# Another order of the same instructions in a linear attention with a two-layer feed-forward behind it

## The chip, the cores and the metric

The kernel runs on one core of a Trainium2 chip. The metric is the device time of one execution in microseconds. A NeuronCore has a matrix engine (TensorE, PE in the profile; its weight loads are PEld), VectorE (DVE), ScalarE (ACT), GpSimd (POOL) and a sync engine (SP) that here only issues DMAs. Each engine takes its own instructions in program order; semaphores hold them to each other.

## The reference

The first half is a linear attention with a decaying state, for 4 batches, 8 heads, 768 positions and a head size of 48:

```
for t in range(S):
    kt, vt, rt, wt = (k[:, :, t], v[:, :, t], r[:, :, t], w[:, :, t])
    cur = np.einsum('bhd,bhe->bhde', u[None] * kt, vt)
    y[:, :, t] = np.einsum('bhd,bhde->bhe', rt, state + cur)
    state = wt[:, :, :, None] * state + np.einsum('bhd,bhe->bhde', kt, vt)
```

The second half takes y as x (3072 rows of 384) through `h = np.maximum(x @ w_in, 0.0)` with w_in of 384 x 2048, and `h * h @ w_out` with w_out of 2048 x 384. All data are float32.

## The kernel before, in words

The sequence is cut into 6 chunks of 128 positions. A unit is one chunk of one batch; c1b3 below stands for chunk 1, batch 3. All weights stay on the chip.

**Weights.** There are 8 blocks, w0 to w7, each with a half of w_in (`wi`, 768 numbers in each of 128 partitions) and one of w_out (`wo`). SP loads them (L416, L418). Each matrix product is made of three: a number is split into a lead, which the fast matrix format holds, and the rest. Per half block that takes one ACT copy (L429), three VectorE operations (shift L433, sign L437, low L442), one ACT copy of the lead (L449) and one subtraction on POOL (L450).

**Attention of a unit.** SP loads w, k, r (L472) and v (L505). From chunk 2 on VectorE transposes blocks (L481, the steps z0 and z1 for two batches together) and SP spreads them into the tile `pt` (L491); before, PE transposes. VectorE makes the running product of w (scan, four of L536), r times it (rt, L554) and three products for k (kn L560, kn2 L561, kq L564). In chunks 1 to 4 the diagonal terms come from POOL (rk L586, ru L588), a VectorE sum (L591), three small VectorE maxima (bh, L594 to L596) and ACT (diag, L632). PE turns k (ktp, L637), and ACT copies it (L639). Then comes one long PE step, "mix" of a unit: L670 (through the state), L679 and L652 (scores and outer products of the next unit), L689. After it VectorE adds the state (S L699, S2 L702) and masks the next unit's scores (mask, L711), ACT and VectorE split the result into lead and rest (x L613, xl L616), SP sends parts to other partitions (L727), and ACT clears the accumulator (zero, L824).

**Feed-forward.** A position in it is a number, two steps of which (28, 30, ...) are one block of 128 of the 2048 hidden columns for four batches (for chunk 1 and part of chunk 0 for two batches). Per block: hp on PE (L862, nine matmuls), g1 on ACT (L867), g2 (ACT L869 in chunk 0, VectorE L871 after), g3 on ACT (L873), g4 on VectorE (L874, the rest of the squared hidden values), and ob on PE (L880, three matmuls per batch). There are two buffers for hp and three for g.

**What sets the order.** Every step is added with its reads and writes (class Plan, `add`). The numbers of all 2451 steps stand in a table ORDER in the order in which they are emitted (`order`, `run`); each engine executes its share in that order. PLACES names a buffer for each slot, FILLS puts idle transposes on PE ahead of some early steps. ORDER, PLACES and FILLS are handed over in one line:

```
P.table = ORDER, PLACES, FILLS
with tc.manual_schedule():
    P.run()
```

Of the kernel before, what the change touches and what calls it, by code (L numbers as in the profile page):

```python
# [96 lines left out]
class Names:  # L97
# [121 lines left out]
)  # L219
FILLS = {  # L220
    17: (3, 'ob', 1), 16: (3, 'ob', 2), 56: (3, 'ob', 1), 57: (4, 'ob', 1), 42: (3, 'ob', 1), 49: (2, 'ob', 1), 83: (3, 'ob', 3), 90: (18, 'ob', 1),
    160: (4, 'ob', 0), 469: (2, 'ob', 0), 128: (2, 'side', 0), 130: (3, 'side', 0), 192: (7, 'side', 0),
}

# [796 lines left out]
```

## Time and profile before

| what | value |
|---|---|
| median of 3 runs | 528.38 us (526.41 to 528.43) |
| the profiled execution | 528.06 us |
| its span, first to last instruction | 526.3 us, mean granted clock 0.992 |
| PE busy | 506.8 us (96%), 5425 matmuls |
| PEld busy | 457.3 us (87%) |
| DVE busy | 368.8 us (70%), 799 instructions |
| ACT busy | 319.0 us (61%) |
| POOL busy | 98.6 us (19%) |

Busy shares are means over the span. VectorE and ScalarE work hardest in the first 130 us, in which the weights are split and chunks 0 and 1 and the start of chunk 2 of the attention are made; PE has no gap in many later stretches. So the question for each stretch is which engine PE waits for there.

### The profile page before, as it was taken

What the parts mean: (1) busy time and instruction counts of PE and PEld (TensorE: products, weight loads), DVE (VectorE), ACT (ScalarE), POOL (GpSimd) and SP (SyncE); (2) the same over time, 40 slices, a digit from 0 to 9 for tenths busy, and PEclk for the clock granted to TensorE, in tenths of its full rate; (3) what the DMA queues carried; (4) which work ended last, traced back from release to release, by engine and by line L of the source; (5) the groups of instructions that cost most, each with busy time, mean ns of one, the idle gap of its engine ahead of it and who ended that gap; (6) DMA issues with size and microseconds to landing.
All of it is one profiled execution on the core that took longest, in us unless ns stands there. A gap on an engine that the chain in (4) does not pass through costs nothing.

```text
span 526.3 us, 13737 instructions
## 1 busy us (share of the span) xinstructions
PE 506.8 (96%) x5425; PEld 457.3 (87%) x5425; DVE 368.8 (70%) x799; ACT 319.0 (61%) x870; POOL 98.6 (19%) x141
## 2 busy tenths in 40 slices
PE   8999998989999999999998999999999999999995
PEld 7888887768999999988987998889988888998894
DVE  6899889999687899878778667678467354333232
ACT  5898888877775867666574556564543353423232
POOL 2025741734204040220403000402100000000000
PEclk9899999998999999999999999999999999999999
DMA  8989799502657756466672481661171010100001
GB/s 164 226 196 232 163 224 203 126 16 48 106 110 97 146 89 105 91 112 105 93 153 32 72 147 18 102 121 40 25 138 36 1 20 6 57 17 0 1 0 65
DMA packets 188312, 48.74 MB, mean 93 GB/s; under 512 B 178001, under 2 KB 183122, under 8 KB 188242
## 3 DMA queue, kind: packets, MB, share of 16 engines
q1 hardware_dynamic: 187664, 47.01, 46.8%
q8 instruction: 44, 0.72, 0.6%
q10 hardware_dynamic: 578, 0.79, 0.4%
q14 instruction: 26, 0.21, 0.1%
HBM read 31.66 MB, written 4.72 MB: 69 GB/s over the span
## 4 chain that ended last, share of the span: by engine, by line
PE 78%; DVE 9%; SPq 6%; DMA 3%; ACT 2%; issue 1%; POOL 0%; DVEq 0%; POOLq 0%
PE ob L880 34%; PE hp L862 33%; PE ob L670 2%; SPq L505 2%; PE ob L689 2%; SPq L416 2%; DMA ri<-in_moe_w_in_dram 2%; PE a L679 2%; DVE q L442 1%; PE a L652 1%; DMA ro<-in_moe_w_out_dram 1%; DVE g L874 1%; SPq L472 1%; PE hp L637 1%; DVE q L437 1%
## 5 line engine op out<-in xcount | busy, mean ns | idle before, releaser
L880 PE MATMUL ob<-wo,g 128*128 128x384 f32 x1152 | 229.5, 342 | 5.3 <-DVE g L874 2.9
L862 PE MATMUL hp<-x,wi 128*128 128x512 f32 (+1 forms) x1062 | 221.9, 354 | 4.0 <-DVE g L874 2.3
L880 PEld LDWEIGHTS ob<-wo,g 128*128 128x128 f32 x1152 | 200.3, 189 | 14.5 <-DVE g L874 3.8
L862 PEld LDWEIGHTS hp<-x,wi 128*128 128x128 f32 x1062 | 174.3, 188 | 30.6 <-DVE g L874 3.3
L871 DVE SCALAR_TENSOR_TENSOR hp<-hp,t 128x512 f32<-128x512 f32 (+1 forms) x96 | 58.1, 606 | 74.1 <-ACT t L867 73.8
L867 ACT ACTIVATE t<-hp 128x512 f32<-128x512 f32 (+1 forms) x118 | 60.9, 517 | 67.1 <-PE hp L862 42.3
L874 DVE TENSOR_TENSOR g<-hp,g 128x512 fp32r<-128x512 f32 (+1 forms) x118 | 68.9, 585 | 37.5 <-ACT g L873 37.0
L873 ACT CAST g<-hp 128x512 fp32r<-128x512 f32 (+1 forms) x118 | 59.6, 507 | 48.9 <-DVE hp L871 47.9
L660 POOL MEMSET S<- 1x1 f32 x20 | 1.8, 88 | 238.9 <-PE ob L670 238.9
L632 ACT ACTIVATE m<-diag,beta 128x64 f32<-128x64 f32 x160 | 40.3, 337 | 2.6 <-DVE beta L595 2.6
L616 DVE SCALAR_TENSOR_TENSOR x<-ob,x 112x128 fp32r<-112x128 f32 x80 | 21.1, 283 | 18.9 <-ACT x L613 16.6
L824 ACT COPY ob<-zero 112x128 f32<-112x128 f32 x80 | 20.6, 268 | 19.1 <-DVE x L616 9.6
L613 ACT ACTIVATE x<-ob 112x128 fp32r<-112x128 f32 x80 | 19.2, 277 | 20.3 <-PE ob L689 14.6
L536 DVE TENSOR_TENSOR_SCAN pt<-pt,zero 112x128 f32<-112x128 f32 x64 | 27.1, 455 | 2.6 <-DMA pt<-st 1.0
L586 POOL TENSOR_TENSOR st<-st 128x384 f32<-128x384 f32 x20 | 22.6, 1134 | 32.8 <-DVE st L481 22.7
L450 POOL TENSOR_TENSOR wi<-q,wi 128x768 fp32r<-128x768 f32 x8 | 17.0, 2128 | 45.1 <-ACT wi L449 32.7
L588 POOL TENSOR_TENSOR st<-st,un 128x384 f32<-128x384 f32 x20 | 21.8, 1096 | 1.2
L481 DVE STREAM_TRANSPOSE st<-st 128x1152 f32<-128x1152 f32 x16 | 21.6, 1362 | 0.0
L554 DVE TENSOR_TENSOR pt<-pt 112x508 f32<-112x508 f32 x24 | 21.0, 877 | 0.6 <-ACT pt L522 0.4
L543 ACT ACTIVATE m<-pt 112x512 f32<-112x512 f32 x24 | 15.2, 632 | 9.1 <-DVE pt L536 7.8
L450 POOL TENSOR_TENSOR wo<-q,wo 128x768 fp32r<-128x768 f32 x8 | 15.7, 1961 | 26.0 <-ACT wo L449 26.0
L561 DVE SCALAR_TENSOR_TENSOR m<-pt,m 112x512 f32<-112x512 f32 x24 | 18.2, 760 | 0.3
(121 smaller groups left out, 542.8 us busy)
## 6 DMA issues: line engine op xcount, KB each, us to landing
pt<-st SPq DMA_DIRECT2D x96, 96.0 KB, 2.9
ro<-in_moe_w_out_dram SPq DMA_DIRECT2D x8, 768.0 KB, 6.0
v<-in_v_dram SPq DMA_DIRECT2D x96, 48.0 KB, 2.8
out_dram<-q SPq DMA_DIRECT2D x20, 192.0 KB, 2.0
ri<-in_moe_w_in_dram SPq DMA_DIRECT2D x32, 96.0 KB, 4.7
ri<-in_moe_w_in_dram SPq DMA_DIRECT2D x8, 384.0 KB, 6.0
st<-in_w_dram SPq DMA_DIRECT2D x8, 384.0 KB, 4.9
st<-in_k_dram SPq DMA_DIRECT2D x8, 384.0 KB, 4.6
```

The costliest lines, as they stand in the source:

```text
L450: P.add("pool", 1.9, rank(8 * k + 5), lambda q=q, tt=tt: G.tensor_tensor(out=tt[:, 1], in0=q.tile, in1=tt[:, 0].bitcast(F32), op=ALU.subtr ...
L481: V.transpose(out=zt[:, i].rearrange("a t p q i -> a t (p q) i"), in_=sv[:, :, i].rearrange("s t p q x -> s t (p q) x"))
L536: lambda p=p: V.tensor_tensor_scan(out=pt[:, 0, p], data0=src(0)[:, p], data1=zero.broadcast_to([HP, C]), initial=1.0, op0=ALU.mult, op1=A ...
L586: P.add("pool", 0.97, rank("rk"), lambda: G.tensor_tensor(out=rk(), in0=rk(), in1=vals(2), op=ALU.mult), r=[(st, ui, 2)], w=[(st, ui, 1)])
L588: P.add("pool", 0.97, rank("ru"), lambda: G.tensor_tensor(out=rk(), in0=rk(), in1=un.rearrange("s (h d) -> s h d", d=D), op=ALU.mult), r=[ ...
L632: A.activation(M.tile[:, o:o + Q], diag2, AF.Copy, scale=beta.tile[:, i:i + 1])
L862: T.matmul(hp.tile[:, 0:n], wi[f][:, wl, kt], xT[:, kt, xl, xs], start=(m == 0), stop=(m == 3 * KT - 1))
L867: P.add("act", 0.49 if full else 0.28, rank("g1"), lambda: A.activation(t(), h(), AF.Relu), r=[hp], w=[(g, 1)])
L871: P.add("dve", 0.605 if full else 0.337, rank("g2"), lambda: V.scalar_tensor_tensor(out=h(), in0=h(), scalar=0.0, in1=t(), op0=ALU.max, op ...
L873: P.add("act", 0.48 if full else 0.26, rank("g3"), lambda: A.copy(out=hi(), in_=h()), r=[hp], w=[(g, 0)])
L874: P.add("dve", 0.605 if full else 0.335, rank("g4"), lambda: V.tensor_tensor(out=lo(), in0=h(), in1=hi().bitcast(F32), op=ALU.subtract), r ...
L880: T.matmul(obs[b][:, 0:DM], g.tile[0][:, gl, o:o + C], wo[f][:, wl], start=(f == 0 and m == 0), stop=(f == NF - 1 and m == 2))
```

## The change

Only the three tables differ. Every step stays on its engine with the same operation and shape; the emission order changes, and with it which buffer a slot gets. The last 690 of the 2451 numbers of ORDER are the same, from the mix of chunk 4, batch 1 on. The steps that follow differ in the first 320 us or so of the program. FILLS has 56 idle transposes in place of 57, at other places. One row of ORDER and the whole of FILLS in the diff:

```
 ORDER = (
-    5, 15, 19, 21, 7, 6, 17, 16, 315, 0, 11, 20, 18, 8, 13, 24, 25, 26, 27, 22, 23, 28, 1, 10, 314, 9, 56, 62, 2, 31, 60, 32, 33, 12, 93, 58, 29, 316, 65, 30,
...
 FILLS = {
-    17: (3, 'ob', 1), 16: (3, 'ob', 2), 56: (3, 'ob', 1), 57: (4, 'ob', 1), 42: (3, 'ob', 1), 49: (2, 'ob', 1), 83: (3, 'ob', 3), 90: (18, 'ob', 1),
-    160: (4, 'ob', 0), 469: (2, 'ob', 0), 128: (2, 'side', 0), 130: (3, 'side', 0), 192: (7, 'side', 0),
+    17: (3, 'ob', 1), 16: (6, 'ob', 2), 56: (4, 'ob', 1), 57: (5, 'ob', 1), 42: (3, 'ob', 1), 81: (5, 'ob', 1), 90: (18, 'ob', 0), 160: (6, 'ob', 0),
+    128: (5, 'ob', 0), 478: (1, 'side', 0),
 }
```

**Place 1, VectorE, about 125 to 134 us.** The rows begin behind the last weight operation of all (L442 on `ro_86`, block w7). L594 to L596 are bh, L561 and L564 are kn2 and kq of c1b3, L699 and L702 add states, the first L874 that reads `g_95` before is g4 at 28, the second is g4 at 30. Before:

```order
L616 SCALAR_TENSOR_TENSOR x_141<-ob_148,x_141 112x128
L561 SCALAR_TENSOR_TENSOR m_163<-pt_136,m_163 112x512
L594 TENSOR_TENSOR beta_178<-beta_178 64x4
L595 TENSOR_TENSOR beta_178<-beta_178 64x4
L596 TENSOR_TENSOR beta_178<-beta_178 64x4
L699 TENSOR_TENSOR S_173<-a_153,S_139 112x96
L699 TENSOR_TENSOR S_173<-a_154,S_139 112x96
L702 TENSOR_TENSOR S_174<-a_154,S_173 112x96
L874 TENSOR_TENSOR g_95<-hp_152,g_95 128x512
L702 TENSOR_TENSOR S_174<-a_153,S_173 112x96
L564 TENSOR_TENSOR pt_136<-pt_136,m_163 112x2x4x64
L874 TENSOR_TENSOR g_99<-hp_151,g_99 128x512
```

Here g4 at 28 stands behind kn2 and bh (then that of c1b2). On the same engine and stretch now, g4 at 28 is the one that reads `g_99`, and g4 at 30 the one that reads `g_95`:

```order
L442 SCALAR_TENSOR_TENSOR q_156<-ro_86,q_156 128x768
L616 SCALAR_TENSOR_TENSOR x_141<-ob_147,x_141 112x128
L699 TENSOR_TENSOR S_173<-a_154,S_139 112x96
L874 TENSOR_TENSOR g_99<-hp_151,g_99 128x512
L594 TENSOR_TENSOR beta_179<-beta_179 64x4
L595 TENSOR_TENSOR beta_179<-beta_179 64x4
L596 TENSOR_TENSOR beta_179<-beta_179 64x4
L561 SCALAR_TENSOR_TENSOR m_164<-pt_136,m_164 112x512
L564 TENSOR_TENSOR pt_136<-pt_136,m_164 112x2x4x64
L874 TENSOR_TENSOR g_95<-hp_152,g_95 128x512
```

The g4 at 28 has moved ahead of bh and kn2; bh (now that of c1b3), kn2 and kq stand behind it and ahead of the turn of k on PE that reads kq.

**Place 2, VectorE, about 280 to 288 us.** L481 are z0 and z1 of chunk 4, batches 2 and 3; L536 are scans of c4b1; the L874 that reads `g_99` before, and `g_95` with hp_151 now, is g4 at 88. Before:

```order
L481 STREAM_TRANSPOSE st_157<-st_158 128x1152
L871 SCALAR_TENSOR_TENSOR hp_151<-hp_151,t_100 128x512
L481 STREAM_TRANSPOSE st_157<-st_158 128x1152
L536 SCALAR_TENSOR_TENSOR pt_135<-pt_135,zero 112x128 x3
L874 TENSOR_TENSOR g_99<-hp_151,g_99 128x512
L616 SCALAR_TENSOR_TENSOR x_141<-ob_148,x_141 112x128
```

Both transposes and three scans stand close ahead of g4 at 88 here. VectorE in the same stretch now:

```order
L871 SCALAR_TENSOR_TENSOR hp_151<-hp_151,t_96 128x512
L711 COPY_PREDICATED m_165<-caus,a_154 128x256
L616 SCALAR_TENSOR_TENSOR x_141<-ob_147,x_141 112x128
L874 TENSOR_TENSOR g_95<-hp_151,g_95 128x512
L616 SCALAR_TENSOR_TENSOR x_168<-ob_150,x_168 112x128
L616 SCALAR_TENSOR_TENSOR x_141<-ob_148,x_141 112x128
L616 SCALAR_TENSOR_TENSOR x_141<-ob_149,x_141 112x128
L481 STREAM_TRANSPOSE st_157<-st_158 128x1152 x2
```

Both transposes have moved behind g4 at 88, the scans further ahead, and the second mask of c3b3 has come to stand ahead of it.

**Place 3, PE, about 109 to 122 us,** between the mix of c1b0 and that of c1b1. L862 are hp at 24 and 26 (here the ninefold groups), L637 is ktp of c1b2, L880 are ob. Before:

```order
L880 MATMUL ob_149<-wo_79,g_97 128x384 x3
L880 MATMUL ob_148<-wo_79,g_97 128x384 x3
L880 MATMUL ob_148<-wo_79,g_95 128x384 x3
L880 MATMUL ob_150<-wo_79,g_95 128x384 x3
L880 MATMUL ob_147<-wo_79,g_95 128x384 x3
L862 MATMUL hp_151<-x_142,wi_81 128x512 x9
L637 MATMUL hp_152<-ident,pt_136 128x112 x4
L880 MATMUL ob_150<-wo_83,g_99 128x384 x3
```

One hp group stands in it here. PE in the same stretch now:

```order
L880 MATMUL ob_150<-wo_79,g_97 128x384 x3
L862 MATMUL hp_151<-x_142,wi_81 128x512 x9
L880 MATMUL ob_150<-wo_79,g_99 128x384 x3
L880 MATMUL ob_148<-wo_79,g_99 128x384 x3
L862 MATMUL hp_152<-x_142,wi_81 128x512 x9
L880 MATMUL ob_147<-wo_79,g_99 128x384 x3
L880 MATMUL ob_147<-wo_83,g_95 128x384 x3
L637 MATMUL hp_151<-ident,pt_136 128x112 x4
L880 MATMUL ob_149<-wo_79,g_99 128x384 x3
```

One hp group, that at 24, has moved from ahead of the mix of c1b0 to behind it, and fewer ob groups stand between the two mixes.

## Rows read from the trace of the kernel before

**Rows 1.** Windows of 20 us: busy of PE, PEld, DVE, ACT, POOL; clock; DMA.
```profile
100.00:120.00 20.00, 17.36 (x205) 14.48 (x205) 19.74 (x32) 16.21 (x42) 10.23 (x8) 0.97 0.06 11
200.00:220.00 20.00, 20.00 (x368) 19.32 (x366) 17.89 (x54) 15.30 (x51) 0.75 (x5) 1.00 0.57 105
```

**Rows 2.** Waits of PE by line and releaser: us in total, times, longest.
```profile
PE ob L880 <- DVE g L874: 2.9, 3, 1.5
...
PE hp L862 <- DMA x<-x: 0.3, 1, 0.3
```

**Rows 3.** Timeline, 115 to 119 us: start, duration, engine line operation, [idle before <-releaser].
```profile
115.77 1.81 DVE L595 TENSOR_TENSOR beta<-beta 64x4 f32<-64x4 f32 x1
...
118.20 0.47 ACT L824 COPY ob<-zero 112x128 f32<-112x128 f32 x2 [2.54 <-DVE x L616]
...
118.52 3.19 PE L880 MATMUL ob<-wo,g 128*128 128x384 f32 x9 [1.78 <-ACT ob L824]
```

**Rows 4.** Windows of 2 us of PE: length, busy, granted clock, DMA.
```profile
120.00:122.00 2.00, 2.00 (x19) 0.50 0.00 0
```

**Rows 5.** Timeline, 124 to 134 us.
```profile
124.87 0.95 DVE L442 SCALAR_TENSOR_TENSOR q<-ro,q 128x768 uint32<-128x768 uint32 x1
...
126.53 0.68 DVE L561 SCALAR_TENSOR_TENSOR m<-pt,m 112x512 f32<-112x512 f32 x1
...
126.77 2.16 POOL L450 TENSOR_TENSOR wo<-q,wo 128x768 fp32r<-128x768 f32 x1 [3.53 <-ACT wo L449]
...
127.22 1.72 DVE L594 TENSOR_TENSOR beta<-beta 64x4 f32<-64x4 f32 x1
...
128.10 0.58 ACT L873 CAST g<-hp 128x512 fp32r<-128x512 f32 x1
...
128.98 0.93 DVE L595 TENSOR_TENSOR beta<-beta 64x4 f32<-64x4 f32 x1
...
129.94 0.93 DVE L596 TENSOR_TENSOR beta<-beta 64x4 f32<-64x4 f32 x1
...
131.49 0.68 DVE L874 TENSOR_TENSOR g<-hp,g 128x512 fp32r<-128x512 f32 x1
...
132.22 1.50 PE L880 MATMUL ob<-wo,g 128*128 128x384 f32 x7 [1.50 <-DVE g L874]
132.25 1.20 DVE L564 TENSOR_TENSOR pt<-pt,m 112x512 f32<-112x512 f32 x1
```

**Rows 6.** Timeline, 281 to 288 us.
```profile
281.81 1.37 DVE L481 STREAM_TRANSPOSE st<-st 128x1152 f32<-128x1152 f32 x1
...
283.10 3.42 DVE L536 TENSOR_TENSOR_SCAN pt<-pt,zero 112x128 f32<-112x128 f32 x3
...
283.27 2.37 PE L862 MATMUL hp<-x,wi 128*128 128x512 f32 x9
...
286.44 0.66 DVE L874 TENSOR_TENSOR g<-hp,g 128x512 fp32r<-128x512 f32 x1
...
287.16 2.36 PE L862 MATMUL hp<-x,wi 128*128 128x512 f32 x9 [1.52 <-DVE g L874]
```

**Rows 7.** Line L595: minimum, median, maximum ns; first and last start.
```profile
L595 DVE TENSOR_TENSOR beta<-beta x20: 155/157/1809, 70.9 to 391.0; 64x4 f32<-64x4 f32 x20
```

**Rows 8.** Line L554, the same columns.
```profile
L554 DVE TENSOR_TENSOR pt<-pt x24: 654/679/2335, 8.5 to 411.3; 112x508 f32<-112x508 f32 x24
```

**Rows 9.** The chain that ended last, 405 to 416 us: start, duration, what.
```profile
409.89 2.10 PE hp L862 x9
412.00 1.04 PE ob L880 x6
```

**Rows 10.** Timeline, 3.5 us: SP issues the first half of a value load.
```profile
3.57 0.77 SPq L505 DMA_DIRECT2D v<-in_v_dram  x1
```

**Rows 11.** Timeline, 108 us: VectorE beside a POOL subtraction.
```profile
108.25 2.30 POOL L450 TENSOR_TENSOR wo<-q,wo 128x768 fp32r<-128x768 f32 x1
...
108.78 2.32 DVE L554 TENSOR_TENSOR pt<-pt 112x508 f32<-112x508 f32 x1
```

199 rows, old and new, of tables (ORDER, PLACES) are left out of this document.

## The prediction, made before the changed kernel ran

> **What bounds the kernel now.** I read the table of busy shares first: PE is busy for nearly the whole span, so what there is to gain lies where PE waits. I then read the 20 us windows for the stretches where it isn't full. From 100 to 120 us PE is busy for 17.36 us and VectorE for 19.74 [rows 1]: VectorE bounds there. From 200 to 220 PE has all 20.00 us [rows 1]; what is gained before 140 us therefore stays gained, since PE itself goes on from there, and what is gained in VectorE or ACT alone in such a stretch is worth nothing. Third, the waits of PE: three on g4 for ob make 2.9 us, and one on the parts that SP sends 0.3 [rows 2]. Last, the timeline around the longest waits, to see what stood ahead of the late instruction on its own engine.
>
> It shows a thing that the shares don't: VectorE is often busy without working. The small maximum L595 takes 0.157 us in the median and 1.81 at its longest [rows 7], in the 115.77 row, in which the clear of the accumulator and then PE follow it late: PE waits 1.78 us there [rows 3]. The product L554 takes 0.68 in the median [rows 8] and 2.32 at 108.78, beside a subtraction of POOL from 108.25 to 110.55 [rows 11]. At 127.22, 128.98 and 129.94 the three maxima of bh take 1.72, 0.93 and 0.93 while POOL has its subtraction of 126.77 and then other work [rows 5]. Those all read two tensors from SBUF. The g4 of 131.49, which takes one of its two from PSUM, needs its normal 0.68 [rows 5]. So it matters what stands behind such an operation.
>
> The Trainium skill, "GPSIMD Engine Reference", Specifications, says that GpSimd shares its SBUF interfaces with VectorE and that instructions with two SBUF inputs contend. The trace agrees (1.72 against 0.157). It speaks against a change that only reorders VectorE: by that rule the loss goes to whichever two-input operation now stands beside POOL. That is the third rival below.
>
> **The change part by part.** No step is added or removed, so every term is a wait that goes or comes.
>
> *A, place 1, 126 to 134 us.* PE waits 1.50 us at 132.22 for g4 at 28 [rows 5]. That g4 starts at 131.49, though its g3 ended at 128.10 + 0.58 = 128.68. Ahead of it stood kn2 (0.68) and bh (1.72 + 0.93 + 0.93 = 3.58 us with the stalls). Both now stand behind it. It can then start when its g3 is done. One ob group less stands ahead of hp at 28 on PE, 1.04/2 = 0.52 us [rows 9], so g3 ends at about 128.2 and g4 at 128.9; PE has other ob groups up to past 130, so this wait goes. Next late is the turn of k in c1b3: it needs bh, kn2 and kq, all behind g4 now. With the stalls of before that makes 3.58 + 0.68 + 1.20 = 5.46 us, ending at 134.4; without, 3 x 0.157 + 0.68 + 0.68 = 1.83 us, ending at 130.7. PE comes to it at about 133.3: from hp at 30's end near 128.1, ten ob groups of 0.52. Between the two ends the wait is 0 to 1.1 us. POOL's 2.16 us subtraction still follows the last weight operation of 124.87, so some stall stays; but part of POOL's work is over by 128.9. I take 0.3. Term A: -1.5 + 0.3 = -1.2 us, between -1.5 and -0.4.
>
> *The stretch 109 to 122 us (place 3).* One hp group of 2.10 us [rows 9] comes in behind the mix of c1b0 and two ob groups (1.04) go. PE has some 1 us more to do there, and the 1.78 us wait for the clear [rows 3] can shrink. I don't count it: VectorE is full there (19.74 of 20), so PE only waits somewhere else until VectorE has split the last weights, and that end is in A. What could change it is the sum of VectorE's stalls, a gain or a loss of one such stall (2.32 - 0.68 = 1.64 us) or more. I take 0, and keep -3.3 to +4.9, two stalls less to three more.
>
> *B, place 2, 281 to 288 us.* hp at 92 needs the buffer that g4 at 88 frees. It starts at 287.16, 3.89 us after hp at 90 (283.27), where a group takes 2.10 [rows 6, 9]: 1.79 lost, of which the row shows 1.52 as wait. Ahead of that g4 (286.44) VectorE had z1 (1.37) and three scans that took 3.42 together [rows 6]. Both transposes go behind g4, the scans further ahead. Ahead of g4 now stand masks and a part of the split of c3b3's result, about 1.5 us from the end of the mix, where PE has hp at 90 and an ob group, 2.10 + 0.52 = 2.62 us. The wait goes: -1.8. What is late next: the second mask of c3b3 now stands close ahead of the mix that reads it, behind kq (0.68) and g2; PE has two ob groups there, 1.04, against VectorE's 1.4 to 2 after kq. That is 0 to 1 us, and is counted in E. Behind it, the transposes are later by a few us for the spread of c4b2, which is wanted after 310 us.
>
> *C, sends of c2b3 at 220 us.* They come earlier on SP; the wait of 0.3 [rows 2] goes: -0.3, between -0.3 and 0.
>
> *D, the start.* On SP one half of the value load of c0b0 now stands ahead of the load of k. It takes 0.77 us on the queue [rows 10]; where that is passed on through a chain that VectorE bounds, it is lost whole. What hides it, if anything, is that the chain may wait longer for the r of the same unit; the rows don't show that. +0.3, between 0 and +0.8. The idle transposes are one fewer, at other places: nothing, as they fill waits.
>
> *E, new tight places.* The masks of c3b3 (0 to 1 us), the two sub-blocks whose ob now comes right behind its g4 near 170 us, and the clears ahead of the last mixes of chunks 1 and 2, each a fraction of a microsecond on either side of zero. Such a place costs at most the 1.50 of A's wait. Taken together: +0.5, between 0 and +1.9.
>
> Sum: -1.2 + 0 - 1.8 - 0.3 + 0.3 + 0.5 = -2.5 us. Against the profiled execution's 528.06 us that is 525.6. It stands 0.3 us under the median of the runs shown (528.38), of which the lowest is 526.41.
>
> **The rivals.** About 0.5%, 2.6 us, is what a measurement of this kernel can tell from no change; so faster is under 525.7, slower over 531.0.
>
> *1. The waits move.* bh, kn2 and kq of c1b3 keep their stalls, the turn of k takes over g4's wait, and E comes with its upper half. A is -0.4, E +1.2: 528.06 - 0.4 - 1.8 - 0.3 + 0.3 + 1.2 = 527.1, no change. For it: five long two-input operations stand in one row beside POOL's subtraction. Against it: g4 at 28 itself is free.
>
> *2. The stretch before 125 us shortens as well.* PE's clock was at half, 0.50 of 2.4 GHz, so 1.2, in the 120 to 122 us window [rows 4], after the waits around 117 us; nine ob matmuls took 3.19 us at 118.52 [rows 3] where nine take 1.57 otherwise (three halves of 1.04) [rows 9]. If the wait for the clear goes with place 3 and VectorE loses a stall less (1.64), then 525.6 - 1.6 - 1.6 = 522.4. For it: the 115.77 stall has no need to stand ahead of the splits of c1b0, and part of them has moved ahead of it. Against it: VectorE remains full, and PE must wait somewhere. The Trainium skill, "TensorE: Matmul & The Clock Gate", Part 1, has the clock fall after idle time; the row agrees, and a wait that is split into shorter ones would then cost no clock.
>
> *3. VectorE's stalls grow (slower).* The place is 80 to 125 us, the price one stall of 1.64 us per two-input operation that newly meets a subtraction of POOL, the point of decision three of them: nothing hides them, because VectorE is full, and the last weight operation with all behind it comes 4.9 us later. Then A's gain is a gain from a later point: 528.06 - 1.2 - 1.8 - 0.3 + 0.3 + 0.5 + 4.9 = 530.5, and 531.4 where E comes with its half of 1.4. For it: in POOL's order the products for chunk 2 now stand ahead of the last subtraction and kn2, kq and a shift follow a low part directly. Against it: r times the product of c1b3, which took 2.32 beside POOL, has moved away from it, and masks, states and g4, which read PSUM, stand beside POOL now.
>
> **How the numbers follow.** Forecast (its own range 523.9 to 527.2): 0.40, of it 0.25 under the bound for faster and 0.15 above. Rival 1: 0.24, no change. Rival 2: 0.18, faster. Rival 3: 0.18, slower. That is faster 0.25 + 0.18 = 0.43, within 0.5% 0.15 + 0.24 = 0.39, slower 0.18. The range goes from 521.2, rival 2 with one stall less again in part, to 531.2, between the two ends of rival 3.
>
> **What would show it.** Right: g4 at 28 starts within 1 us of its g3's end and PE has no wait of over 0.5 us between 128 and 134 us; hp at 92 follows hp at 90 without a wait on g4; the wait on sent parts near 220 us is gone. A wrong: a wait of 1 us or more before the turn of k of c1b3, with bh or kn2 beside POOL. B wrong: a wait on a mask in the mix of c3b3. Rival 2: the clock at full from 116 to 122 us. Rival 3: the last L442 ends later than 125.8 us, and more or longer two-input operations than before between 80 and 125 us. The forecast as a whole is wrong where the gain lies outside 100 to 290 us, or where PE loses its full windows after 140 us.

## The result, and the profile after

The changed kernel took 520.62 us in the median of 4 runs (519.12 to 520.96), the kernel before 528.01 (4 runs). The ratio is 0.986, with a 95% interval of 0.9831 to 0.9889: 7.4 us less. The prediction was 525.6 with a range from 521.2, so it had the sign, but a third of its size, and its range ended 0.6 us above the result.

The page of the changed kernel: its span, and the granted clock in 40 slices, which stays at full up to the last (0.9 and more of it is a 9).

```profile
span 518.9 us, 13715 instructions
...
PEclk9999999999999999999999999999999999999998
```

Windows of 20 us, columns as in [rows 1], of the changed kernel:

```profile
80.00:100.00 20.00, 20.00 (x175) 18.13 (x175) 19.54 (x38) 19.83 (x48) 11.49 (x7) 1.00 0.90 186
100.00:120.00 20.00, 17.10 (x318) 14.16 (x317) 19.87 (x35) 14.18 (x35) 8.28 (x10) 1.00 0.13 22
200.00:220.00 20.00, 20.00 (x249) 18.43 (x253) 16.43 (x43) 12.32 (x43) 1.83 (x4) 1.00 0.54 99
```

and the one of before that the prediction did not look at:

```profile
80.00:100.00 20.00, 17.70 (x154) 15.00 (x153) 19.80 (x36) 17.17 (x37) 6.17 (x4) 1.00 1.00 196
```

From 80 to 100 us PE was busy for 17.70 us and is now for 20.00. From 100 to 120 it still has gaps (17.10, where it was 17.36), with VectorE as full as before. From 200 to 220 us PE is full in both [rows 1].

Two of PE's waits in the changed kernel (total us, times, longest):

```profile
PE ob L880 <- DVE g L874: 2.3, 2, 1.6
PE ob L880 <- ACT ob L824: 1.7, 2, 1.3
```

The wait on the sent parts [rows 2] is gone. So is the single 1.8 us wait for the clear [rows 3], for which two of 1.7 together stand now. The waits of ob on g4 went from 2.9 to 2.3 [rows 2].

To see where the time came from, I take a step's start on PE less the nominal time of all PE steps before it (per kind of step, the lower fifth of the distances between starts). The difference is what PE has lost up to there, in us; below, that is the loss or gain by landmarks:

| step on PE | before | changed | gained so far |
|---|---|---|---|
| scores of c0b2 (32 us) | 13.1 | 11.9 | 1.2 |
| turn of c1b2 (83 us) | 22.0 | 20.0 | 2.0 |
| mix of c1b0 (107 us) | 26.0 | 21.2 | 4.8 |
| mix of c1b1 (122 us) | 31.2 | 25.2 | 6.0 |
| mix of c1b2 (139 us) | 33.5 | 26.2 | 7.3 |
| mix of c1b3 (157 us) | 33.9 | 27.8 | 6.1 |
| mix of c3b3 (281 us) | 37.6 | 31.7 | 5.9 |
| mix of c4b0 (317 us) | 39.9 | 32.4 | 7.5 |
| last ob | 44.4 | 36.9 | 7.5 |

Four of the 7.5 us come between 83 and 122 us, where the prediction counted nothing. They are of two kinds. From 83 to 107 us before loses 4.0 us and the changed kernel 1.2, and the same reckoning gives 4.0 in e1, e3, e5, e7, e8 and e12 below, which have the old order there: these 2.8 us belong to the order. From 107 to 122 us before loses 5.2 and the changed kernel 4.0, but e8 and e5, with the old order and no fall of the clock there, lose 3.8 each: this part isn't the order's but that of the half clock in the profile of before [rows 4]. The 1.2 us at 32 us are no more than profiles of one order differ by: the scores of c0b2 start at 32.6 us in before, at 30.9 in e3, 30.4 in e7 and 31.8 in e8, which have the same instructions up to there, and at 31.4 in the changed kernel.

What happened at 83 us shows the mechanism. Before (timeline: start, duration, engine, line):

```profile
83.18 1.96 POOL L450 TENSOR_TENSOR wi<-q,wi 128x768 fp32r<-128x768 f32 x1 [3.57 <-DMA st<-in_k_dram]
...
83.35 2.33 DVE L554 TENSOR_TENSOR pt<-pt 112x508 f32<-112x508 f32 x1
...
87.02 2.37 PE L862 MATMUL hp<-x,wi 128*128 128x512 f32 x9 [1.38 <-DVE pt L536]
...
87.47 0.68 DVE L874 TENSOR_TENSOR g<-hp,g 128x512 fp32r<-128x512 f32 x1
...
93.64 2.19 DVE L561 SCALAR_TENSOR_TENSOR m<-pt,m 112x512 f32<-112x512 f32 x1
```

rt of c1b1 starts 0.17 us after POOL's subtraction, and lasts until 85.68, 0.54 us past that subtraction's end at 85.14. The four scans, kq and g4 at 16 follow it in VectorE's order, and hp at 18 on PE, whose buffer the scans free, starts 1.38 us late. The same happens again at 93.64, where kn2 of c1b1 lasts 2.19 us beside the subtraction of 93.44; by the reckoning of the table PE loses 1.55 us behind the first and 1.18 behind the second. The changed kernel:

```profile
80.56 0.68 DVE L554 TENSOR_TENSOR pt<-pt 112x508 f32<-112x508 f32 x1
...
81.42 2.14 POOL L450 TENSOR_TENSOR wi<-q,wi 128x768 fp32r<-128x768 f32 x1 [3.78 <-ACT wi L449]
...
82.01 1.37 DVE L536 TENSOR_TENSOR_SCAN pt<-hp,zero 112x128 f32<-112x128 f32 x4 [0.18 <-PE hp L519]
...
83.92 2.26 PE L862 MATMUL hp<-x,wi 128*128 128x512 f32 x9
```

rt stands ahead of the subtraction and takes 0.68. What stands beside the subtraction are scans that read PSUM, at their normal pace, and PE has no wait ahead of its hp.

The last weight operation (L442) ended at 125.82 [rows 5] and now ends at 120.48, 5.34 us earlier. Summed over VectorE up to there, the time above an instruction's usual one (the lower quartile of its line and shape) fell from 16.4 to 13.0 us, and VectorE's idle time from 12.8 to 10.5. What is left is nearly the same (96.7 and 97.0 us), so the stalls make 3.4 and the idle time 2.3 of what was saved. Of the stalls, 15.8 and 12.5 us fall on instructions that overlap one of POOL. Not all of those are the weight subtraction: in before it is the products L586 and L588 from 56 to 62 and from 100 to 106 us.

At place 1, A's g4 at 28 (121.51) starts 0.04 us after the end of its g3 (120.89 + 0.58), as foreseen, and the next late thing is kq, as foreseen:

```profile
119.53 0.95 DVE L442 SCALAR_TENSOR_TENSOR q<-ro,q 128x768 uint32<-128x768 uint32 x1
...
120.89 0.58 ACT L873 CAST g<-hp 128x512 fp32r<-128x512 f32 x1
...
121.44 5.38 PE L880 MATMUL ob<-wo,g 128*128 128x384 f32 x30
121.51 0.69 DVE L874 TENSOR_TENSOR g<-hp,g 128x512 fp32r<-128x512 f32 x1 [0.66 <-ACT g L873]
...
122.29 1.84 POOL L450 TENSOR_TENSOR wo<-q,wo 128x768 fp32r<-128x768 f32 x1 [2.70 <-ACT wo L449]
122.42 1.72 DVE L595 TENSOR_TENSOR beta<-beta 64x4 f32<-64x4 f32 x1
...
125.04 0.67 DVE L561 SCALAR_TENSOR_TENSOR m<-pt,m 112x512 f32<-112x512 f32 x1
125.06 1.53 POOL L586 TENSOR_TENSOR st<-st 128x384 f32<-128x384 f32 x1
...
125.75 1.39 DVE L564 TENSOR_TENSOR pt<-pt,m 112x512 f32<-112x512 f32 x1
...
127.20 0.60 PE L637 MATMUL hp<-ident,pt 112*128 112x112 f32 x4 [0.38 <-DVE pt L564]
```

bh is stretched to 1.72 + 0.94, kq to 1.39, and the turn of k waits 0.38 us. Between them kn2 begins 0.02 us ahead of a product of POOL and keeps its usual time; here the product is the longer one (1.53, median 1.01). At place 2 hp at 92 follows hp at 90 with an ob group between, without a wait ([rows 6]: 1.52):

```profile
277.35 2.37 PE L862 MATMUL hp<-x,wi 128*128 128x512 f32 x9
...
280.09 2.26 PE L862 MATMUL hp<-x,wi 128*128 128x512 f32 x9
```

What was moved away there was stretched too. The scans of [rows 6] took 3.42 us for three, where one takes 0.41 in the median; they read two tensors in SBUF, and POOL had its products beside them. Before:

```profile
283.07 1.00 POOL L586 TENSOR_TENSOR st<-st 128x384 f32<-128x384 f32 x1
```

### The profile page after: what moved, and what is told of

The parts are those of the page before. It is cut to its first block, busy times and chain, and to the rows that moved or that the text cites. A ratio compares the mean times of both kernels' runs of the same rounds, so it can differ in the third digit from the quotient of the medians.

```text
span 518.9 us, 13715 instructions
## 1 busy us (share of the span) xinstructions
PE 503.9 (97%) x5424; PEld 455.7 (88%) x5424; DVE 363.8 (70%) x799; ACT 315.7 (61%) x870; POOL 99.3 (19%) x141
## 4 chain that ended last, share of the span: by engine, by line
PE 79%; DMA 8%; DVE 5%; SPq 3%; ACT 2%; issue 1%; POOL 0%; ACTq 0%; POOLq 0%
PE hp L862 35%; PE ob L880 34%; DMA ri<-in_moe_w_in_dram 3%; PE ob L670 2%; DMA st<-in_k_dram 2%; DMA ro<-in_moe_w_out_dram 2%; PE ob L689 2%; PE a L679 2%; SPq L505 1%; PE a L652 1%; PE hp L637 1%; SPq L472 1%; DVE q L442 1%; SPq L416 1%; DVE beta L595 1%
## 5 line engine op out<-in xcount | busy, mean ns | idle before, releaser
L880 PE MATMUL ob<-wo,g 128*128 128x384 f32 x1152 | 227.7, 340 | 3.9 <-DVE g L874 2.3
L862 PE MATMUL hp<-x,wi 128*128 128x512 f32 (+1 forms) x1062 | 222.0, 355 | 1.5 <-DVE g L874 1.3
L880 PEld LDWEIGHTS ob<-wo,g 128*128 128x128 f32 x1152 | 199.2, 188 | 12.7 <-DVE g L874 2.9
L862 PEld LDWEIGHTS hp<-x,wi 128*128 128x128 f32 x1062 | 174.5, 188 | 28.3 <-DVE g L874 2.9
L874 DVE TENSOR_TENSOR g<-hp,g 128x512 fp32r<-128x512 f32 (+1 forms) x118 | 69.1, 586 | 38.4 <-ACT g L873 37.6
L586 POOL TENSOR_TENSOR st<-st 128x384 f32<-128x384 f32 x20 | 22.9, 1144 | 16.9 <-DVE st L481 16.1
L536 DVE TENSOR_TENSOR_SCAN pt<-pt,zero 112x128 f32<-112x128 f32 x64 | 25.0, 419 | 1.5 <-DMA v<-in_v_dram 1.3
L450 POOL TENSOR_TENSOR wi<-q,wi 128x768 fp32r<-128x768 f32 x8 | 15.0, 1876 | 43.7 <-DMA ri<-in_moe_w_in_dram 26.7
L588 POOL TENSOR_TENSOR st<-st,un 128x384 f32<-128x384 f32 x20 | 22.6, 1133 | 1.1
L481 DVE STREAM_TRANSPOSE st<-st 128x1152 f32<-128x1152 f32 x16 | 21.5, 1361 | 0.0
L450 POOL TENSOR_TENSOR wo<-q,wo 128x768 fp32r<-128x768 f32 x8 | 16.5, 2057 | 24.8 <-ACT wo L449 16.0
L560 DVE TENSOR_TENSOR pt<-pt,m 112x512 f32<-112x512 f32 x24 | 17.6, 732 | 2.3 <-ACT Ec L559 2.0
L554 DVE TENSOR_TENSOR pt<-pt 112x508 f32<-112x508 f32 x24 | 18.4, 765 | 0.2
L561 DVE SCALAR_TENSOR_TENSOR m<-pt,m 112x512 f32<-112x512 f32 x24 | 17.1, 711 | 0.3
```

What stands on the lines that cost most here:

```text
L450: P.add("pool", 1.9, rank(8 * k + 5), lambda q=q, tt=tt: G.tensor_tensor(out=tt[:, 1], in0=q.tile, in1=tt[:, 0].bitcast(F32), op=ALU.subtr ...
L481: V.transpose(out=zt[:, i].rearrange("a t p q i -> a t (p q) i"), in_=sv[:, :, i].rearrange("s t p q x -> s t (p q) x"))
L536: lambda p=p: V.tensor_tensor_scan(out=pt[:, 0, p], data0=src(0)[:, p], data1=zero.broadcast_to([HP, C]), initial=1.0, op0=ALU.mult, op1=A ...
L586: P.add("pool", 0.97, rank("rk"), lambda: G.tensor_tensor(out=rk(), in0=rk(), in1=vals(2), op=ALU.mult), r=[(st, ui, 2)], w=[(st, ui, 1)])
L588: P.add("pool", 0.97, rank("ru"), lambda: G.tensor_tensor(out=rk(), in0=rk(), in1=un.rearrange("s (h d) -> s h d", d=D), op=ALU.mult), r=[ ...
L862: T.matmul(hp.tile[:, 0:n], wi[f][:, wl, kt], xT[:, kt, xl, xs], start=(m == 0), stop=(m == 3 * KT - 1))
```

## The experiments

Each was timed against runs of before on the same chip. A comparison with 12 runs has an interval of about 0.2 to 0.3% on each side, one with 6 to 8 runs 0.3 to 0.4%. The mean granted clock differs between the runs of two kernels too, and that is worth up to 2 us here (last experiment); where it bears on a reading it is given.

**First hybrids: stretches of one order in the other.** The tables were spliced: one order up to a step, then the rest of the steps in the other's sequence.

```
e1:  ORDER = changed[up to scores of c0b2] + rest in old order;  FILLS = changed
e2:  ORDER = old[up to split of w4] + changed[up to mix of c1b2] + rest in old order;  FILLS = old
e3:  ORDER = old[up to mix of c3b2] + rest in changed order;  FILLS = old
```

> The changed order and its idle transposes up to the scores of c0b2 (about 32 us), the old order from there. By landmarks of PE (time less the nominal work done) the changed kernel was 1.2 us ahead there, 2.0 us at 83 us, 6.0 at 121, 7.3 at 139, 5.9 at 281 and 7.5 at the end. Theory (the gains of the stretches add up, since PE or VectorE is full in between): -0.8 to -1.6 us against before, and the clock at full from 16 to 20 us. Rival (VectorE's queue behind 32 us absorbs it): within 0.4 us of before.

> The old order up to the split of w4's first half (about 72 us), the changed one up to the mix of c1b2 (139 us), the old one behind. Theory (most of the gain is made here, because VectorE's two-input operations stand less often beside POOL's): -4 to -5.5 us, and the last weight operation (L442) ends 3 to 4.5 us earlier than 125.8 us. Rival (the gain needs the earlier start, which feeds VectorE sooner): -2 us or less.

> The old order up to the mix of c3b2 (271 us), the changed one behind. Theory (step B of the prediction): hp at 92 follows hp at 90 without its wait, -1.3 to -1.9 us. Rival (the wait moves to the mix of c4b0): within 0.5 us.

Measured: e1 532.32 us against 528.20 (ratio 1.008, 1.0047 to 1.0113), slower; e2 531.40 (1.0049, 1.0019 to 1.0079), slower; e3 525.88 (0.9964, 0.9934 to 0.9993), as the theory had it. (In e1, and in e6 below, idle transposes of the changed table come at a step where the old order already has an accumulator in use, which changes numbers of the result, not the instructions.) The loss by landmarks tells why the first two failed. e1 is 1.1 us ahead of before at 32 us, and loses 3 us in the next 10, in the seam: the two orders had done different steps there. e2 lost 4.3 us between 70 and 83 us in its seam and 2.9 at the second; but between the turn of c1b2 and the mix of c1b1 it lost 5.1 us, as the changed kernel does (5.2), where before loses 9.2 and e8, without the fall of the clock, 7.8. So the order inside that stretch makes the difference, and my expectation for the whole time was wrong since it left out the seam. A time shift does not help: e1 meets the same long operations as before, one for one (1.56 us of wait at 86, 1.19 at 97, 2.02 at 117).

**The change in three pieces, with better seams.** The changeovers were put where the sets of steps done differ in 3 and 6 steps of 2451.

```
e5:  ORDER = changed[0:180] + rest in old order;                      FILLS of the changed steps up to there
e6:  ORDER = old[0:181] + changed[up to its 626th] + rest in old order;  FILLS of the changed steps in the middle
e7:  ORDER = old[0:626] + rest in changed order;                      FILLS = old
```

> The first hybrids changed over where the two orders had done different work, and lost 3 to 4 us in the seam itself. This one changes over where the sets of steps done differ in 3 of 2451: the changed order and its idle transposes up to the masks of c0b2 (35 us), the old order behind. Theory (the stretches add up): -0.8 to -1.5 us, all of it before 35 us, the clock at full from 16 to 20 us, and the same waits as before between 83 and 133 us. Rival: VectorE's queue absorbs it, within 0.5 us.

> The old order up to the masks of c0b2 (35 us), the changed one from there to the mix of c1b1 (115 to 122 us), the old one behind (seams that differ in 3 and in 6 steps). By landmarks of PE the changed kernel gains 6.0 - 1.2 = 4.8 us in this stretch. Theory (the gain is in this stretch by its own order, as the stretch from 83 to 122 us lost 5.1 us in the first hybrid where it lost 9.2 before): -3.5 to -5.5 us. Rival (it takes the whole): -2 us or less.

> The old order up to the mix of c1b1 (122 us), the changed one behind (the seam differs in 6 steps). It holds all three terms that the prediction counted (A, B and C). By landmarks of PE the changed kernel gains 7.5 - 6.0 = 1.5 us behind this point: 1.3 up to the mix of c1b2, then 1.2 given back up to that of c1b3, and 1.6 at 281 to 316 us. Theory: -1 to -2 us. Rival (A's place is gained only because VectorE comes there earlier): -0.5 us, or nothing.

Measured against 528.55: e5 526.16 (0.9956, 0.9941 to 0.9972), e6 523.62 (0.9917, 0.9891 to 0.9943), e7 525.59 (0.9952, 0.9934 to 0.9971). In us: -2.3, -4.4, -2.5. The middle piece is the largest, as expected. The two others came out above their expected ranges, and the product of the ratios (0.9826) lies just outside the whole's interval (0.9831 to 0.9889). The clock is counted in each piece: the means were 0.996, 0.996 and 0.995 against 0.993, which by the slope found below is 1.3, 1.0 and 0.8 us. Without it the pieces are 1.0, 3.4 and 1.7 us, 6.1 together, where the whole has 6.3: the gain is made in all three, a little over half of it between 35 and 122 us.

**Two stalls alone.**

```order
 L437 SCALAR_TENSOR_TENSOR q_155<-ri_76,q_155 128x768
+L554 TENSOR_TENSOR pt_135<-pt_135 112x4x127
 L442 SCALAR_TENSOR_TENSOR q_155<-ri_76,q_155 128x768
 L874 TENSOR_TENSOR g_97<-hp_152,g_97 128x512
 L561 SCALAR_TENSOR_TENSOR m_167<-pt_135,m_167 112x512
-L554 TENSOR_TENSOR pt_135<-pt_135 112x4x127
```

The second move takes kn2 of c1b1 (L561) ahead of an L437 and a g4 in the same way.

> The old order with two VectorE operations moved: rt of c1b1 (2.33 us beside POOL at 83.35) ahead of the low part of w5's first half, and kn2 of c1b1 (2.19 at 93.64) ahead of the sign step of w6's first half. Nothing else moves. Theory (the stalls themselves made PE wait, 1.55 us at 85 and 1.18 at 96): both take about 0.7 us and the time falls by 1.5 to 3 us. Rival (the stall only moves to the next two-input operation, or PE's waits have another cause): within 0.5 us.

Measured: 526.63 us against 528.20 (0.9977, 0.9953 to 1.0002), -1.2 us, at the edge of what can be told and between the theory's range and the rival's. VectorE in it:

```profile
81.05 0.68 DVE L554 TENSOR_TENSOR pt<-pt 112x508 f32<-112x508 f32 x1
...
85.98 0.68 DVE L874 TENSOR_TENSOR g<-hp,g 128x512 fp32r<-128x512 f32 x1
...
93.14 2.34 DVE L442 SCALAR_TENSOR_TENSOR q<-ri,q 128x768 uint32<-128x768 uint32 x1
```

rt now takes 0.68, g4 at 16 starts at 85.98 instead of 87.47, and the wait of hp at 18 is gone. The second move did what the rival said: kn2 is short, and the low part L442 that stands beside the subtraction now takes 2.34. One of two stalls (1.65 us) removed, one wait of 1.55 us gone, and 1.2 us gained up to the mix of c1b0 by landmarks: of this stall most is passed on to PE.

**Step A alone.**

```order
-L561 SCALAR_TENSOR_TENSOR m_163<-pt_136,m_163 112x512
+L699 TENSOR_TENSOR S_173<-a_153,S_139 112x96
+L699 TENSOR_TENSOR S_173<-a_154,S_139 112x96
+L702 TENSOR_TENSOR S_174<-a_154,S_173 112x96
+L874 TENSOR_TENSOR g_95<-hp_152,g_95 128x512
 L594 TENSOR_TENSOR beta_178<-beta_178 64x4
 L595 TENSOR_TENSOR beta_178<-beta_178 64x4
 L596 TENSOR_TENSOR beta_178<-beta_178 64x4
-L699 TENSOR_TENSOR S_173<-a_153,S_139 112x96
-L699 TENSOR_TENSOR S_173<-a_154,S_139 112x96
-L702 TENSOR_TENSOR S_174<-a_154,S_173 112x96
-L874 TENSOR_TENSOR g_95<-hp_152,g_95 128x512
+L561 SCALAR_TENSOR_TENSOR m_163<-pt_136,m_163 112x512
```

> Before with step A alone: kn2 of c1b3 and bh of c1b2 stand behind g4 at 28 on VectorE, nothing else moves. By the prediction PE's wait of 1.50 us for that g4 goes and -1.2 us stay. Theory now: VectorE has the same work and the same stalls up to kq of c1b3, which PE needs 1.3 us after that wait; the wait only moves to the turn of k: within 0.5 us of before, with a wait of 1 us or more ahead of the turn of k of c1b3.

Measured: 526.30 against 528.55 (0.997, 0.9949 to 0.9992). Its trace shows the wait moved, as the theory said:

```profile
126.89 0.69 DVE L874 TENSOR_TENSOR g<-hp,g 128x512 fp32r<-128x512 f32 x1 [1.25 <-ACT g L873]
...
129.80 1.32 DVE L564 TENSOR_TENSOR pt<-pt,m 112x512 f32<-112x512 f32 x1
...
131.17 0.60 PE L637 MATMUL hp<-ident,pt 112*128 112x112 f32 x4 [1.44 <-DVE pt L564]
```

g4 at 28 is done at 127.58, and the turn of k waits 1.44 us for kq instead. Between the mixes of c1b1 and c1b2 it loses 2.0 us where before loses 2.3. By the ratio the whole is 1.6 us (0.4 to 2.7) less, more than the 0.5 expected. Its mean granted clock over its runs was 0.996, that of the runs of before 0.993, which by the slope found below is 1.1 us of it; so this half of A alone is worth little, 0.3 by landmarks. It is half of A because PE's order is the old one: six ob groups (18 matmuls, 3.29 us from 126.45) stand between hp at 30 and the turn of k, where the changed kernel has ten (the x30 row above).

**The cause taken away.** POOL's subtraction for w5 to w7 became a fill.

```
-  G.tensor_tensor(out=tt[:, 1], in0=q.tile, in1=tt[:, 0].bitcast(F32), op=ALU.subtract)
+  ... if g < 5 else G.memset(tt[:, 1].bitcast(F32), 0.0)
```

> Before, with POOL's subtraction for weight blocks w5 to w7 (six half blocks, 83 to 129 us) replaced by a fill with zeros, which reads nothing: the rest part of these weights is left out of the result. Everything else and the order stay. Theory (VectorE's operations with two SBUF inputs stand still while POOL's subtraction runs): the long ones at 83, 93, 108, 115 and 127 us take their normal time, the last L442 ends 4 us or more before 125.8 us, and the time falls by 3.5 to 6 us. Rival (the changed kernel gains by PE's own order, and the stalls cost nothing of their own): within 1 us of before.

> The changed kernel with the same six subtractions replaced by fills with zeros (the rest part of w5 to w7 is left out). Theory: it has fewer such stalls to lose (1.2 at 104, 1.6 at 111 and 2.3 at 122 to 125 us stand beside these subtractions), so it falls by 1 to 3.5 us from 520.6, and the gap between the two orders shrinks from 7.4 to 2 to 5 us. Rival (order of PE): both fall alike and the gap stays near 7.4.

Measured against 528.22: e9 519.06 us (0.9826, 0.9788 to 0.9863), e10 515.89 (0.9767, 0.973 to 0.9804). By the medians the old order falls by 9.2 us, the changed one, from 520.62, by 4.7, and the gap goes from 7.4 to 3.2. Both fell more than expected. The mean clock was 0.998 over the runs of both, against 0.992 before, which by the slope found below is 2.1 us of the 9.2. Why the rest is above the expectation wasn't taken apart. That PE itself waited for the subtraction is not the reason: the profile of before has 0.3 us of such a wait in all (L880 on L450). The old order without the cause:

```profile
82.55 0.74 POOL L450 MEMSET wi<- 128x768 f32 x1 [2.74 <-DVE q L442]
...
82.96 0.68 DVE L561 SCALAR_TENSOR_TENSOR m<-pt,m 112x512 f32<-112x512 f32 x1
...
83.56 0.68 DVE L554 TENSOR_TENSOR pt<-pt 112x508 f32<-112x508 f32 x1
...
86.02 0.68 DVE L874 TENSOR_TENSOR g<-hp,g 128x512 fp32r<-128x512 f32 x1
...
111.71 0.16 DVE L595 TENSOR_TENSOR beta<-beta 64x4 f32<-64x4 f32 x1
...
118.21 0.95 DVE L442 SCALAR_TENSOR_TENSOR q<-ro,q 128x768 uint32<-128x768 uint32 x1
```

The long operations take 0.68 and 0.16, g4 at 16 comes at 86.02, and the last L442 ends at 119.16 instead of 125.82. kn2 at 82.96 stands beside the fill and isn't stretched: it is not POOL being busy that counts, but POOL's subtraction, which reads SBUF. PE loses 1.5 us from 83 to 107 us here (4.0 in before) and 0.4 from 107 to 122 (5.2): the stalls cost PE in both stretches, and the changed order took away those of the first alone.

**The other waits of the changed kernel.** In it PE still waits behind two stretched operations:

```profile
104.23 1.90 DVE L564 TENSOR_TENSOR pt<-pt,m 112x512 f32<-112x512 f32 x1
...
108.08 0.96 PE L880 MATMUL ob<-wo,g 128*128 128x384 f32 x4 [1.59 <-DVE g L874]
...
111.15 1.77 DVE L595 TENSOR_TENSOR beta<-beta 64x4 f32<-64x4 f32 x1
...
113.35 0.47 ACT L824 COPY ob<-zero 112x128 f32<-112x128 f32 x2 [2.35 <-DVE x L616]
...
113.86 1.31 PE L880 MATMUL ob<-wo,g 128*128 128x384 f32 x6 [1.29 <-ACT ob L824]
```

kq (L564), stretched to 1.90, stands ahead of g4 at 22; bh (1.77) ahead of the split results that the clears need. Three moves on VectorE: g4 at 22 ahead of kq, bh behind the split results, the state sums and z1, kn2 and kq of c1b3 right behind the last L442:

```order
+L874 TENSOR_TENSOR g_99<-hp_152,g_99 128x512
 L564 TENSOR_TENSOR pt_136<-pt_136,m_166 112x2x4x64
 L433 TENSOR_SCALAR q_155<-q_155 128x768
...
-L874 TENSOR_TENSOR g_99<-hp_152,g_99 128x512
...
 L442 SCALAR_TENSOR_TENSOR q_156<-ro_86,q_156 128x768
+L561 SCALAR_TENSOR_TENSOR m_164<-pt_136,m_164 112x512
+L564 TENSOR_TENSOR pt_136<-pt_136,m_164 112x2x4x64
```

> The changed kernel with three more moves on VectorE: g4 at 22 ahead of kq of c1b2, a shift, two masks and a state sum; bh of c1b2 (1.77 us beside POOL at 111) behind the next split results and z1; kn2 and kq of c1b3 right behind the last weight operation, ahead of the 1.8 us in which POOL isn't yet at its subtraction. In the changed kernel PE waits 1.97 us at 106 for g4 at 22, 1.5 at 112 for the clear that bh delays, 0.55 at 126 for kq. Theory (what stands behind a two-input operation is what counts, so each of the waits goes): -1.5 to -4 us against the changed kernel, 516.5 to 519. Rival (VectorE is full, so the waits return at the last weight split): within 1 us of 520.6.

Measured: 516.97 us (6 runs, 516.52 to 517.57) against 528.22 (0.9786, 0.975 to 0.9822): 11.3 us under before and 3.6 under the changed kernel, which was timed in other runs against the same kernel before. It beats both. Of the 3.6, the clock (0.998 against 0.996) makes 0.8 by the slope found below. bh and kq of c1b3 are short, kq of c1b2 still lasts 1.31, now behind g4 at 22, and the last L442 ends at 117.89, 2.6 us earlier than in the changed kernel:

```profile
112.29 0.16 DVE L595 TENSOR_TENSOR beta<-beta 64x4 f32<-64x4 f32 x1
...
116.95 0.94 DVE L442 SCALAR_TENSOR_TENSOR q<-ro,q 128x768 uint32<-128x768 uint32 x1
...
118.53 0.69 DVE L564 TENSOR_TENSOR pt<-pt,m 112x512 f32<-112x512 f32 x1
...
119.31 1.84 POOL L450 TENSOR_TENSOR wo<-q,wo 128x768 fp32r<-128x768 f32 x1 [2.31 <-ACT wo L449]
...
123.67 0.55 PE L637 MATMUL hp<-ident,pt 112*128 112x112 f32 x4
```

kq ends 0.1 us before the subtraction starts. The turn of k waits for nothing, and the waits of ob on g4 and on the clear shrink (2.3 and 1.7 in the changed kernel):

```profile
PE ob L880 <- DVE g L874: 0.7, 1, 0.7
...
PE ob L880 <- ACT ob L824: 0.3, 1, 0.3
```

**The clock.** Before, with other counts of idle transposes: `16: (3, 'ob', 2)` to `(6, 'ob', 2)`, `56: (3, ..)` to `(4, ..)`, `57: (4, ..)` to `(5, ..)`. These are the changed kernel's own counts for the three steps.

> Before with more idle transposes at the start (6 for 3, 4 for 3, 5 for 4 ahead of three of the first turns), the order unchanged. In the profile of before PE's clock is at half from 16 to 20 us, in those of three other kernels with the same start it isn't, so it comes and goes by run. Theory (fuller PE work ahead makes the fall at 16 us rarer): the mean granted clock over the runs rises from 0.993 by 0.001 to 0.003, and the time falls by 0.4 to 1.2 us (0.38 us per 0.001 over 60 runs of before). Rival (the fall depends on the waits at 12 to 16 us, which stay): no difference in clock or time beyond 0.4 us.

Measured: 526.08 against 528.22 (0.9956, 0.9931 to 0.9981), with a mean clock over the runs of 0.997 against 0.992. Both moved the way of the theory and by more than it expected: 2.1 us, of which the clock's slope accounts for 1.8. So a gain of the size of e5's (2.3), which has these counts as well, is had without any new order. The windows of 2 us of before, of the changed kernel and of e8, whose instructions up to 126 us are those of before (length, PE busy, granted clock, DMA):

```profile
16.00:18.00 2.00, 2.00 (x15) 0.55 0.56 107
18.00:20.00 2.00, 2.00 (x32) 0.60 0.97 179
```

```profile
16.00:18.00 2.00, 2.00 (x35) 1.00 1.34 220
118.00:120.00 2.00, 2.00 (x10) 1.00 0.71 105
```

```profile
16.00:18.00 2.00, 1.99 (x23) 1.00 0.74 102
118.00:120.00 2.00, 2.00 (x36) 1.00 0.00 0
```

The profile of before has two stretches at half clock, 16 to 20 us and 118 to 122 [rows 4]; e8 with the same instructions there has none. They come and go from run to run, but not alike everywhere: of the eight profiles with the old order from 83 to 122 us, six have a fall that begins between 117 and 120 us (not e5 and e8), and of the changed kernel, e10 and e11 none has one ahead of 500 us, while e2 and e6, with its order in that stretch, have one at 115 and at 110 us. Over 60 runs of before the mean clock is 0.993, between 0.987 and 0.999, and the time falls by 0.38 us per 0.001 (correlation -0.83). The four runs of the changed kernel have 0.996. By that slope about 1.1 us of the 7.4 are clock.

## Why the prediction was wrong, point by point

**The step that failed** is what the prediction put at 0 ahead of 122 us, and two terms are in it.

The first is what VectorE's stalls cost PE. The prediction named this mechanism, priced it (1.64 us a stall) and kept -3.3 as an end, but it read it for "the stretch 109 to 122 us" alone, took 0 there, since "VectorE is full there (19.74 of 20), so PE only waits somewhere else until VectorE has split the last weights", and has no term at all for 83 to 107 us. There PE's loss fell from 4.0 to 1.2 us. The two waits that went stood behind the stretched rt at 83.35 and kn2 at 93.64, which it never looked up, although the rows showed L554 at its longest. e6 places the gain in the middle piece; e4 removes one of the two waits by moving VectorE's operation alone; e9 removes both by taking the subtraction away. For 107 to 122 us itself the 0 came out (4.0 us lost in the changed kernel, 3.8 in e8 with the old order), but its reason did not hold: a full engine was taken for one whose end cannot move. Part of its busy time was waiting, and the last split ended 5.34 us earlier.

The second is the idle transposes, which the prediction took as "nothing, as they fill waits". Three of the new counts alone take 2.1 us off before (e12, 1.0 to 3.6), nearly all of it by the clock; by the changed kernel's own mean clock it is about 1.1 us here.

The Trainium skill, "SBUF — State Buffer", Terms, has VectorE and GpSimd share a port pair under a lock for a whole instruction, the loser blocked. The traces agree: bh in [rows 5] ends at 128.94, where the subtraction that began at 126.77 ends. The pairs that collide in before could be read off its trace with their prices, 2.33 - 0.68 us at 83.35 and 2.19 - 0.68 at 93.64; which pairs the new order would bring together could only be estimated. The prediction drew on the rule only for a warning.

**Term D** was wrong in sign: +0.3 against -1.2 by landmarks and -2.3 in e5. A cost of the value load ahead of k doesn't show: the scores of c0b2 start at 31.4 us in the changed kernel, within the 30.4 to 32.8 of profiles with the old queue. What came instead is the clock, at half from 16 to 20 us in before and at full in the changed kernel: four of the eight profiles with the old counts of idle transposes at the start have that fall (before, e2, e4, e9), and none of the six with the new counts.

**Term A** held, in size and in mechanism: -1.2 was foreseen and -1.3 is seen between the mixes of c1b1 and c1b2, with 0.38 us of wait ahead of the turn of k where 0.3 was taken. Both of its moves are needed. With g4 moved alone (e8) the wait goes over to kq; with ten ob groups ahead of the turn, as the term had it, PE comes late enough. e7 agrees: it has the old order up to the mix of c1b1 and the changed one behind, nine groups there, and no wait at the turn although kq lasts 2.21 us.

**Term B** was right: -1.8 against -1.6 by landmarks, and -1.9 us in e3 (0.4 to 3.5, of which 0.7 by the clock's slope). It took the scans' 3.42 us as given; they were stretched by POOL's products, the mechanism of the result once more. **Term C** was right, the wait is gone. **Term E** held: 1.2 us are given back between 139 and 157 us, within the 0 to 1.9 kept, where 0.5 was taken.

**Rival 2**, with 0.18, came nearest (522.4). Its sign, the clock at full from 116 to 122 us, is there; its wait for the clear did not go, it became two waits of 1.7 us together. The clock's falls belong to runs and not only to the order; one profile of before with two of them looked like a property of the kernel. **Rival 3** had the mechanism and the place (80 to 125 us) of the largest gain with the sign turned.

## What to carry to other kernels

Where an engine bounds a stretch, compare each instruction's longest duration with its median before calling the engine's time fixed; what stands out is a wait inside the instruction, and its price falls on whatever the order put behind it. Beside a POOL operation on SBUF put VectorE instructions that read PSUM, and move the pairs of SBUF operands ahead of it or the urgent result ahead of them: three such moves gave another 3.6 us, 0.8 of it by the clock. A hybrid of two orders needs a seam where both have done the same steps, and a clock event in one profile needs a second profile before it is argued from.

## What the runs showed of the hardware

- A VectorE operation of 0.16 us with two SBUF inputs lasted up to 1.81 beside a POOL subtraction of 1.8 to 2.3 us. Beside a POOL fill of 0.74 us, which reads nothing, kn2 took its usual 0.68 (e9, 82.96).
- Two SBUF inputs are not the whole rule here: the shift L433, which reads one tensor, lasted 1.36 us at 56.44 in before, beside POOL's L586, where 0.55 is its median. Transposes (L481), sums (L591) and everything that reads PSUM kept their time beside POOL.
- In one profile of before the clock fell to half in two stretches, in e8 with the same instructions up to 126 us in neither. A 0.001 in the mean clock of a run stood for 0.38 us.
- POOL pays too: L588 took 1.62 us at 101 us in before, where VectorE had L437 and L442 on SBUF beside it, and 1.00 at 286, beside a g4 that reads PSUM. Where kn2 began 0.02 us ahead of it (125.04, changed kernel), POOL's L586 took 1.53 and kn2 its usual time; where POOL began first, as at 83.18, VectorE's operation was the longer one.
